# A state-space layer beside a gated feed-forward on one core: skip term from TensorE to VectorE, two chunks' layer norm from VectorE to ScalarE and GpSimd

## The chip, the core and the metric

The kernel runs on one core of a Trainium2 chip, in one launch. The metric is the device time of a run in microseconds (us). The engines are named as the profile names them: PE is TensorE (matmuls; PEld are its weight loads), DVE is VectorE, ACT is ScalarE, POOL is GpSimd, and SP is SyncE, which here only issues DMAs.

## The reference

The input `x` has 2048 rows (time steps) of 512 features. Each row is normalized to zero mean and unit variance, giving `xn`. Three things are added:

```
def _A_ref(x, ...):                       # called with xn
    Lam_bar = exp(dt * Lam)               # complex, one per state (512 states)
    Bu = einsum("bld,pd->blp", x, B_bar)
    for t in range(L): h = Lam_bar * h + Bu[:, t, :]
    y = 2.0 * einsum("blp,dp->bld", hseq, Cmat).real + x * Dskip
def _B_ref(x, w_gate, w_up, w_down):      # called with xn; F = 1376
    return (silu(x @ w_gate) * (x @ w_up)) @ w_down
return x + _A_ref(xn, ...) + _B_ref(xn, ...)
```

The part that the change is about is `x + xn * Dskip`, called the skip term here: per element one multiplication by a factor that depends on the feature alone, and one addition. Inputs, weights and the output are bf16.

## The kernel before

**Tiles and chunks.** A tile is 128 rows of `x`; there are 16 tiles (0 to 15) and four chunks of four tiles. `x_sb` holds all of `x` in SBUF for the whole run. `xn_sb` holds eight normalized tiles: tile a lies in slot a mod 8, so tiles 8 to 11 overwrite tiles 0 to 3. `xnT` holds the transposed normalized tiles of two chunks; chunk 2 overwrites chunk 0. PSUM has eight banks of 128x512 fp32, and `next_bank` hands out the one that has been idle longest. Every group of four 128x512 matmuls needs one bank, which comes free when ACT has copied the result to SBUF.

**Work of a chunk.** For a chunk c the functions do the following.

- `ln_chunk` normalizes its tiles. `ln_stats` lets DVE compute mean and variance (`bn_stats` L507, `bn_aggr` L509, plus eps L511) and POOL the power -0.5 (L513). In chunks 0 and 1 DVE then applies them (L518). In chunks 2 and 3 (`ln_norm_act`) DVE forms -mean*rstd (L522) and ACT applies both (L524, tasks xn8 to xn15).
- `xt_chunk_dma` transposes the chunk by one DMA on SP's queue (L407, tasks xTd1 to xTd3). Chunk 0 is transposed by PE. A DMA that transposes waits for all DMAs named before it in the code, and those named after it wait for it.
- `ssm_b_chunk` multiplies by B (L821); ACT copies the results to `u_sb` (L828, L830; tasks uev_re, uev_im).
- `ffn_gate` and `ffn_up` (L741) do 11 blocks of the hidden layer; ACT computes silu into `sg` (L754, six slots) and copies the other factor into `uf` (L805, three slots; tasks uev), and DVE multiplies them into `hT` (L807, tasks hmul).
- `ssm_elem_chunk` rotates, scans (L860) and rotates back on DVE, ending in `hss` (L875, tasks h).
- `wprep_C`, once, prepares the output matrix `W12` from C on ACT (L713, L715; tasks wev) and DVE (L717, L720).
- `dc_chunk` adds up the output of each tile in a PSUM bank: phase A is 11 matmuls of the down projection (L909, mm_dA), phase B eight matmuls of hss by W12 (L925, mm_dB). Then DVE adds what is left, into `osb` (L933 or L936, tasks oadd), and a DMA stores it.

**The skip term** is made in two ways. For tiles 0 to 7 (`rs_dve_from=8`) PE multiplies the transposed tile by a diagonal matrix of Dskip, four 128x128 matmuls more in phase A (L912); the diagonals `diagD` are built by DVE at the start from a row of Dskip that ACT's queue loads (L498). The last addition reads `x_sb` (L933). For tiles 8 to 15 `resid_tile` lets DVE compute `xn * dsk + x` in place in `xn_sb` (L596, L598; tasks rs1 and rs2) and the last addition reads `xn_sb` (L936). `dsk` is Dskip on all partitions, the last of the loads.

**The order on each engine.** The code names tasks with what they read and write. `_schedule` then lays them out before the launch: PE and SP keep the order of the code, while ACT, DVE and POOL get, again and again, the task that can start first; among those that can start within 200 ns of it the one with the longest path of costs to the end of the program. The costs are estimates in the code (`est=`); a DMA is reckoned with 2 us and its bytes at 330 per ns. The result is a fixed queue for each engine: an instruction whose data are late holds up all that stand behind it on that engine.

```
                ests = [(est_start(t, e), t) for t in cands]
                tmin = min(x[0] for x in ests)
                for (s_, t) in ests:
                    if s_ <= tmin + slack:
```

**The order of the code** around the change is: chunk 0's `ssm_elem_chunk`, `ln_chunk(2)`, `wprep_C`, all of chunk 1's matmuls, `ln_chunk(3)`, phase A of chunk 0, the transpose of chunk 2, phase B of chunk 0, then chunk 2's `ssm_b_chunk`, and so on with chunk 1's output and chunk 3. The transpose of chunk 2 stands behind phase A since the diagonal matmuls still read chunk 0 in `xnT`.

Of the kernel before, what the change touches and what calls it, by code (L numbers as in the profile page):

```python
# [24 lines left out]
    rs_dve_from=8,  # L25
# [226 lines left out]
def bass_parallel_sum__ssm_conv_s5__swiglu_ffn__prompt_kernel(  # L252
# [32 lines left out]
    with es:  # L285
        block = es.enter_context(nc.Block())

        def sb(name, shape, dt):
            return es.enter_context(nc.sbuf_tensor(name, shape, dt))
# [34 lines left out]
        wtmp = scrC[:, 0:2048].rearrange("p (k d) -> p k d", k=4)  # L324
        vq = sb("vq", [128, NU, 2, 2, CH], B16)
# [8 lines left out]
        praw = sb("praw", [128, 4, PT], B16)  # L334
        prow = sb("prow", [4, 4, 128], B16)
        ecst = sb("ecst", [128, PT], F32)
        diagD = sb("diagD", [128, KT, 128], B16)
# [85 lines left out]
        def pload(name, slot, src):  # L423
            dma(name, prow[:, slot, :], src.rearrange("(a p) -> a p", p=128), [("prow", slot)], 1024, eng="act")
# [3 lines left out]
        pload("ld_dskp", 3, A_Dskip)  # L428
# [57 lines left out]
        def params_t(ks):  # L486
            slot = next_tr()

            def tr(e, slot=slot):
                for k in ks:  # L490
                    inst = e.transpose(out=ptr[:, slot, 4 * k:4 * k + 4], in_=prow[0:4, k, :], identity=ident[0:4, 0:4])
                return inst
            g.add("pe", tr, reads=[("prow", k) for k in ks] + [("ident",)], writes=BK(slot), name="parT%d" % ks[0], est=30 * len(ks), ninst=len(ks))
            g.add("dve", lambda e, slot=slot: e.tensor_copy(out=praw[:, ks[0]:ks[-1] + 1].rearrange("p k a -> p (k a)"), in_=ptr[:, slot, 4 * ks[0]:4 * ks[-1] + 4]),
                  reads=BK(slot), writes=[("praw", k) for k in ks], name="parTev%d" % ks[0], est=80, prio=5000.0)
            if 3 in ks:
                for kt in range(KT):
                    g.add("dve", lambda e, kt=kt: e.tensor_scalar(out=diagD[:, kt, :], in0=ident[:], scalar1=praw[:, 3, kt:kt + 1], scalar2=None, op0=ALU.mult),  # L498
                          reads=[("praw", 3), ("ident",)], writes=[("diagD", kt)], name="diagD%d" % kt, est=90)
# [6 lines left out]
        def ln_stats(a, order=False):  # L506
            ln_bn[a] = g.add("dve", lambda e, a=a: e.bn_stats(out=st[:, a, :], in_=x_sb[:, a, :]),  # L507
                             reads=[("x", a)], writes=[("st", a)], name="bnst%d" % a, est=640)
            ln_ag[a] = g.add("dve", lambda e, a=a: e.bn_aggr(out=mv[:, a, :], in_=st[:, a, :]),  # L509
                             reads=[("st", a)], writes=[("mv", a)], name="bnag%d" % a, est=90)  # L510
            ln_ve[a] = g.add("dve", lambda e, a=a: e.tensor_scalar(out=ve[:, a:a + 1], in0=mv[:, a, 1:2], scalar1=EPS, scalar2=None, op0=ALU.add),  # L511
                             reads=[("mv", a)], writes=[("ve", a)], name="ve%d" % a, est=70)
            g.add("pool", lambda e, a=a: e.tensor_tensor(out=rstd[:, a:a + 1], in0=ve[:, a:a + 1], in1=mhalf[:, a:a + 1], op=ALU.pow),  # L513
                  reads=[("ve", a), ("mhalf",)], writes=[("rstd", a)], name="rstd%d" % a, est=600, prio=(3000.0 if a < 4 else 0.0))

        def ln_scale(a, norm_act):
            if not norm_act:
                ln_xn[a] = g.add("dve", lambda e, a=a: e.tensor_scalar(out=xn_sb[:, a % NXN, :], in0=x_sb[:, a, :], scalar1=mv[:, a, 0:1], scalar2=rstd[:, a:a + 1],  # L518
                                                                        op0=ALU.subtract, op1=ALU.mult),
                                  reads=[("x", a), ("mv", a), ("rstd", a)], writes=[("xn", a % NXN)], name="xn%d" % a, est=350)  # L520
            else:
                g.add("dve", lambda e, a=a: e.scalar_tensor_tensor(out=nmr[:, a:a + 1], in0=mv[:, a, 0:1], scalar=-1.0, in1=rstd[:, a:a + 1], op0=ALU.mult, op1=ALU.mult),  # L522
                      reads=[("mv", a), ("rstd", a)], writes=[("nmr", a)], name="nmr%d" % a, est=70)
                g.add("act", lambda e, a=a: e.activation(out=xn_sb[:, a % NXN, :], in_=x_sb[:, a, :], func=AF.Identity, scale=rstd[:, a:a + 1], bias=nmr[:, a:a + 1]),  # L524
                      reads=[("x", a), ("rstd", a), ("nmr", a)], writes=[("xn", a % NXN)], name="xn%d" % a, est=710)

        def ln_tile(a, norm_act):
            ln_stats(a)
            ln_scale(a, norm_act)

        def ln_head():
            for a in range(4):
                ln_stats(a)
            for a in range(4):
                ln_scale(a, False)
            seq = [ln_bn[0], ln_ag[0], ln_ve[0], ln_bn[1], ln_ag[1], ln_xn[0], ln_ve[1], ln_xn[1], ln_bn[2], ln_ag[2], ln_ve[2], ln_bn[3], ln_ag[3], ln_ve[3], ln_xn[2], ln_xn[3]]
            for p, q in zip(seq, seq[1:]):
                if p not in q.deps:
                    q.odeps.add(p)

# [6 lines left out]
        def ln_chunk(c):  # L547
            for a in range(4 * c, 4 * c + 4):
                ln_tile(a, _CFG["ln_norm_act"][c])
# [45 lines left out]
        def resid_tile(a):  # L595
            g.add("dve", lambda e, a=a: e.tensor_tensor(out=xn_sb[:, a % NXN, :], in0=xn_sb[:, a % NXN, :], in1=dsk[:], op=ALU.mult),  # L596
                  reads=[("xn", a % NXN), ("dsk",)], writes=[("xn", a % NXN)], name="rs1_%d" % a, est=340)
            g.add("dve", lambda e, a=a: e.tensor_tensor(out=xn_sb[:, a % NXN, :], in0=xn_sb[:, a % NXN, :], in1=x_sb[:, a, :], op=ALU.add),  # L598
                  reads=[("xn", a % NXN), ("x", a)], writes=[("xn", a % NXN)], name="rs2_%d" % a, est=340)
# [157 lines left out]
        def ffn_gate_quarters(c, tiles):  # L757
# [21 lines left out]
            params_t([0, 1, 2, 3])  # L779
# [111 lines left out]
        def dc_chunk(c, mid=None, split_last=False):  # L891
# [10 lines left out]
            for (lt, c0, nc_), bk in zip(items, banks):  # L902
                dg = (4 * c + lt < _CFG["rs_dve_from"])
                assert not (dg and nc_ != 512)

                def mmA(e, bk=bk, lt=lt, hb=hb, c=c, c0=c0, nc_=nc_, dg=dg):
                    for i in range(FT):
                        fs = fsz[i]
                        inst = e.matmul(pbank[:, bk, 0:nc_], lhsT=hT[0:fs, hb, i, lt * 128:(lt + 1) * 128], rhs=wd[0:fs, i, c0:c0 + nc_], start=(i == 0), stop=False)  # L909
                    if dg:  # L910
                        for kt in range(KT):
                            inst = e.matmul(pbank[:, bk, kt * 128:(kt + 1) * 128], lhsT=xnT[:, c % 2, lt, kt, :], rhs=diagD[:, kt, :], start=False, stop=False)  # L912
                    return inst
                g.add("pe", mmA, reads=[("hT", hb, i) for i in range(FT)] + [("wd", 0), ("wd", 1)] + (XN(c, lt) + [("diagD", kt) for kt in range(KT)] if dg else []),
                      writes=BK(bk), name="mm_dA%d_%d" % (4 * c + lt, c0), est=FT * (216 if nc_ == 512 else 110) + (KT * 60 if dg else 0), ninst=FT + (KT if dg else 0))
            if mid is not None:
                mid()
            for (lt, c0, nc_), bk in zip(items, banks):
# [13 lines left out]
                if a < _CFG["rs_dve_from"]:  # L932
                    g.add("dve", lambda e, bk=bk, a=a, os_=os_, c0=c0, nc_=nc_: e.tensor_tensor(out=osb[:, os_, 0:nc_], in0=pbank[:, bk, 0:nc_], in1=x_sb[:, a, c0:c0 + nc_], op=ALU.add),  # L933
                          reads=BK(bk) + [("x", a)], writes=[("osb", os_)], name="oadd%d_%d" % (a, c0), est=(660 if nc_ == 512 else 360))
                else:
                    g.add("dve", lambda e, bk=bk, a=a, os_=os_, c0=c0, nc_=nc_: e.tensor_tensor(out=osb[:, os_, 0:nc_], in0=pbank[:, bk, 0:nc_], in1=xn_sb[:, a % NXN, c0:c0 + nc_], op=ALU.add),  # L936
                          reads=BK(bk) + [("xn", a % NXN)], writes=[("osb", os_)], name="oadd%d_%d" % (a, c0), est=(660 if nc_ == 512 else 360))
# [20 lines left out]
        ssm_elem_chunk(0, u0)  # L958
        ln_chunk(2)
# [4 lines left out]
        for i in range(FT):  # L964
            ffn_gate(1, i)
            ffn_up(1, i)
        ln_chunk(3)
        dc_chunk(0, mid=lambda: xt_chunk_dma(2))
# [5 lines left out]
        dc_chunk(1, mid=lambda: xt_chunk_dma(3))  # L974
# [5 lines left out]
        for a in range(_CFG["rs_dve_from"], NT):  # L980
            resid_tile(a)
# [62 lines left out]
```

## Time and profile before

| | |
|---|---|
| time, median of 3 runs | 183.77 us (183.62 to 183.89) |
| the profiled execution's own time | 183.74 us |
| its span, first to last instruction | 182.0 us |
| granted clock of PE | 0.999 |
| busy: PE / DVE / ACT / POOL | 177.6 / 167.5 / 87.4 / 26.2 us |
| diagonal matmuls, L912 | 32, in eight sets of four |
| `bn_stats`, L507 | 16, 683 ns each |
| ACT applying the norm, L524 | 8, 803 ns each |
| DVE's skip term, L596 and L598 | 8 and 8, 418 and 419 ns each |

Times within the execution are counted from the first instruction. The mean duration of an instruction includes the part in which the next one on the same engine already runs, so the distance from one start to the next is shorter: eight results copied one after the other by ACT stand about 0.48 us apart, though each takes 0.6 us.

### The profile page before, as it was taken

What the parts mean: (1) busy time and instruction counts of PE and PEld (TensorE: products, weight loads), DVE (VectorE), ACT (ScalarE), POOL (GpSimd) and SP (SyncE); (2) the same over time, 40 slices, a digit from 0 to 9 for tenths busy, and PEclk for the clock granted to TensorE, in tenths of its full rate; (3) what the DMA queues carried; (4) which work ended last, traced back from release to release, by engine and by line L of the source; (5) the groups of instructions that cost most, each with busy time, mean ns of one, the idle gap of its engine ahead of it and who ended that gap; (6) DMA issues with size and microseconds to landing.
All of it is one profiled execution on the core that took longest, in us unless ns stands there. A gap on an engine that the chain in (4) does not pass through costs nothing.

```text
span 182.0 us, 2595 instructions
## 1 busy us (share of the span) xinstructions
PE 177.6 (98%) x943; PEld 87.0 (48%) x943; DVE 167.5 (92%) x359; ACT 87.4 (48%) x155; POOL 26.2 (14%) x37
## 2 busy tenths in 40 slices
PE   8899999999999999999999999999999999999994
PEld 3684444444444454444444455444444444444643
DVE  3799889999999998999999999999999999999933
ACT  3249987966798308057766480026667620000000
POOL 3597775000000004000000130000000000000000
PEclk9999999999999999999999999999999999999999
DMA  5993665669400000630000000620000000010202
GB/s 123 318 382 88 117 135 78 120 157 359 131 0 4 0 0 0 122 114 0 0 0 0 0 4 0 115 101 15 0 4 2 0 2 0 0 32 0 86 29 86
DMA packets 23404, 12.39 MB, mean 68 GB/s; under 512 B 15104, under 2 KB 23392, under 8 KB 23392
## 3 DMA queue, kind: packets, MB, share of 16 engines
q1 hardware_dynamic: 23360, 12.23, 25.3%
q8 instruction: 7, 0.11, 0.3%
q14 instruction: 5, 0.04, 0.1%
q10 hardware_dynamic: 32, 0.00, 0.0%
HBM read 6.46 MB, written 2.10 MB: 47 GB/s over the span
## 4 chain that ended last, share of the span: by engine, by line
PE 93%; DVE 3%; DMA 1%; POOL 1%; issue 0%; DVEq 0%
PE pb L741 39%; PE pb L909 21%; PE pb L925 15%; PE pb L821 15%; PE pb L768 1%; DMA x_sb<-in_A_x_dram 1%; DVE st L507 1%; PE pb L912 1%; DVE xn_sb L518 1%; POOL rstd L513 1%; POOL sm L643 1%; DVE mv L509 0%; DVE diagD L498 0%; DVE osb L936 0%; PE pb L580 0%
## 5 line engine op out<-in xcount | busy, mean ns | idle before, releaser
L741 PE MATMUL pb<-xnT,wu 128*128 128x512 bf16 (+1 forms) x176 | 43.7, 379 | 0.0
L909 PE MATMUL pb<-wd,hT 128*128 128x512 bf16 (+3 forms) x187 | 39.7, 367 | 0.0
L860 DVE TENSOR_TENSOR_SCAN vq<-sm,car,vq 128x512 bf16<-128x512 f32 x32 | 39.5, 1269 | 0.1
L741 PE MATMUL pb<-xnT,wg 128*128 128x512 bf16 (+1 forms) x152 | 38.4, 379 | 0.0
L805 ACT ACTIVATE uf<-pb 128x512 bf16<-128x512 f32 (+1 forms) x44 | 26.0, 605 | 16.1 <-DVE hT L807 9.3
L925 PE MATMUL pb<-W,hss 128*128 128x512 bf16 (+1 forms) x136 | 28.3, 366 | 0.0
L821 PE MATMUL pb<-xnT,BT 128*128 128x512 bf16 x128 | 28.1, 379 | 0.0
L741 PEld LDWEIGHTS pb<-xnT,wu 128*128 128x128 bf16 (+1 forms) x176 | 17.6, 100 | 20.1
L909 PEld LDWEIGHTS pb<-wd,hT 128*128 128x128 bf16 (+1 forms) x187 | 18.0, 98 | 18.5
L754 ACT ACTIVATE sg<-pb 128x512 bf16<-128x512 f32 (+1 forms) x38 | 22.6, 606 | 7.1 <-PE pb L741 6.9
L741 PEld LDWEIGHTS pb<-xnT,wg 128*128 128x128 bf16 (+1 forms) x152 | 15.3, 101 | 17.6
L513 POOL TENSOR_TENSOR rstd<-ve,mhalf 128x1 f32<-128x1 f32 x16 | 9.6, 616 | 76.1 <-DVE ve L511 76.1
L925 PEld LDWEIGHTS pb<-W,hss 128*128 128x128 bf16 x136 | 13.2, 98 | 13.9
L821 PEld LDWEIGHTS pb<-xnT,BT 128*128 128x128 bf16 x128 | 12.5, 98 | 15.1
L807 DVE TENSOR_TENSOR hT<-sg,uf 128x512 bf16<-128x512 bf16 (+1 forms) x44 | 18.4, 424 | 1.3 <-ACT uf L805 0.8
L828 ACT ACTIVATE u_sb<-pb 128x512 bf16<-128x512 f32 x16 | 9.5, 596 | 17.2 <-PE pb L821 17.2
L507 DVE BATCH_NORM_STATS2 st<-x_sb 128x6 f32<-128x512 bf16 x16 | 10.2, 683 | 3.0 <-DMA x_sb<-in_A_x_dram 3.0
L830 ACT ACTIVATE u_sb<-pb 128x512 bf16<-128x512 f32 x16 | 9.6, 598 | 3.2 <-PE pb L821 3.2
L866 DVE TENSOR_TENSOR scrA<-vq,cosT 128x1024 bf16<-128x1024 bf16 x16 | 10.9, 684 | 0.0
L870 DVE TENSOR_TENSOR scrA<-vq,sin 128x1024 bf16<-128x1024 bf16 x16 | 10.9, 684 | 0.0
L854 DVE TENSOR_TENSOR scrA<-u_sb,sin 128x1024 bf16<-128x1024 bf16 x16 | 10.9, 682 | 0.0
L851 DVE TENSOR_TENSOR scrA<-u_sb,cosT 128x1024 bf16<-128x1024 bf16 x16 | 10.9, 680 | 0.0
(74 smaller groups left out, 143.2 us busy)
## 6 DMA issues: line engine op xcount, KB each, us to landing
out_dram<-osb SPq DMA_DIRECT2D x15, 128.0 KB, 1.7
x_sb<-in_A_x_dram SPq DMA_DIRECT2D x3, 512.0 KB, 7.5
wd<-in_B_w_down_dram SPq DMA_DIRECT2D x1, 1280.0 KB, 7.1
wg<-in_B_w_gate_dram SPq DMA_DIRECT2D x2, 384.0 KB, 4.6
wu<-in_B_w_up_dram SPq DMA_DIRECT2D x1, 768.0 KB, 6.9
wg<-in_B_w_gate_dram SPq DMA_DIRECT2D x1, 608.0 KB, 7.9
wu<-in_B_w_up_dram SPq DMA_DIRECT2D x1, 608.0 KB, 9.0
x_sb<-in_A_x_dram SPq DMA_DIRECT2D x4, 128.0 KB, 3.0
```

Of the source, the lines that this page charges most:

```text
L507: ln_bn[a] = g.add("dve", lambda e, a=a: e.bn_stats(out=st[:, a, :], in_=x_sb[:, a, :]), reads=[("x", a)], writes=[("st", a)], name="bnst% ...
L513: g.add("pool", lambda e, a=a: e.tensor_tensor(out=rstd[:, a:a + 1], in0=ve[:, a:a + 1], in1=mhalf[:, a:a + 1], op=ALU.pow), reads=[("ve", ...
L741: inst = e.matmul(pbank[0:fs, bk, :].rearrange("p (j t) -> p j t", j=4), lhsT=w[:, kt, i * 128:i * 128 + fs], rhs=xnT[:, c % 2, :, kt, :], ...
L754: g.add("act", lambda e, sl=sl, bk=bk, fs=fs: e.activation(out=sg[0:fs, sl, :], in_=pbank[0:fs, bk, :], func=AF.Silu), reads=BK(bk), write ...
L805: g.add("act", lambda e, ul=ul, bk=bk, fs=fs: e.activation(out=uf[0:fs, ul, :], in_=pbank[0:fs, bk, :], func=AF.Identity), reads=BK(bk), w ...
L807: g.add("dve", lambda e, sl=sl, ul=ul, fs=fs, i=i, hb=hb: e.tensor_tensor(out=hT[0:fs, hb, i, :], in0=sg[0:fs, sl, :], in1=uf[0:fs, ul, :] ...
L821: inst = e.matmul(pbank[:, bk, :].rearrange("p (j t) -> p j t", j=4), lhsT=BT[:, ri, kt, pt * 128:(pt + 1) * 128], rhs=xnT[:, c % 2, :, kt ...
L851: g.add("dve", lambda e, sl=sl, U=U, Cb=Cb: e.tensor_tensor(out=pr2[:, sl, 0], in0=U, in1=Cb, op=ALU.mult), reads=ru + rdt, writes=[("pr", ...
L854: g.add("dve", lambda e, sl=sl, Usw=Usw, S2=S2: e.tensor_tensor(out=pr2[:, sl, 1], in0=Usw, in1=S2, op=ALU.mult), reads=ru + rdt, writes=[ ...
L860: g.add("dve", lambda e, sl=sl, ri=ri, pt=pt, rr=rr, c=c: e.tensor_tensor_scan(out=vq[:, sl, 1, ri, :], data0=rr[:, pt:pt + 1].to_broadcas ...
L909: inst = e.matmul(pbank[:, bk, 0:nc_], lhsT=hT[0:fs, hb, i, lt * 128:(lt + 1) * 128], rhs=wd[0:fs, i, c0:c0 + nc_], start=(i == 0), stop=F ...
L925: inst = e.matmul(pbank[:, bk, 0:nc_], lhsT=hss[:, hb, pt, ri, lt * 128:(lt + 1) * 128], rhs=W12[:, ri, pt, c0:c0 + nc_], start=False, sto ...
```

## The change

The diagonal matrices go, with their load, their building and the 32 matmuls. `resid_chunk` does the skip term of all 16 tiles on DVE, now with its sum written into `x_sb`, so all last additions read `x_sb`. Since chunk 2's tiles overwrite chunk 0's in `xn_sb`, chunk 0's skip term is named ahead of `ln_chunk(2)`, and chunk 1's ahead of `ln_chunk(3)`. In chunks 2 and 3 the sums come from ACT: one pass that adds up the tile, one that squares and adds up, both with a sum per row (`accum_out`) and a written tile `junk` that nobody reads; POOL does the small steps between, and ACT applies the norm as before. The transposes of chunks 2 and 3 are named ahead of `dc_chunk` and no longer in its middle.

```diff
-    rs_dve_from=8,
+        junk = sb("junk", [128, 512], B16)
-        diagD = sb("diagD", [128, KT, 128], B16)
-        pload("ld_dskp", 3, A_Dskip)
-            if 3 in ks:
-                for kt in range(KT):
-                    g.add("dve", ... diagD[:, kt, :] = ident * praw[:, 3, kt] ...)
...
+        def ln_tile_act(a):
+            jk = junk[:]
+            g.add("act", lambda e, a=a: e.activation(out=jk, in_=x_sb[:, a, :], func=AF.Identity, accum_out=mv[:, a, 0:1]),
+                  reads=[("x", a)], writes=[("mv", a), ("junk",)], name="lsum%d" % a, est=750)
+            g.add("pool", ... nmr = mv * (-1.0 / D) ...,           name="nmean%d" % a, est=150)
+            g.add("act", lambda e, a=a: e.activation(out=jk, in_=x_sb[:, a, :], func=AF.Square, bias=nmr[:, a:a + 1], accum_out=mv[:, a, 1:2]),
+                  reads=[("x", a), ("nmean", a)], writes=[("ss", a), ("junk",)], name="lsq%d" % a, est=750)
+            g.add("pool", ... ve = mv * (1.0 / D) + EPS ...,       name="ve%d" % a, est=150)
+            g.add("pool", ... rstd = ve ** mhalf ...,              name="rstd%d" % a, est=600)
+            g.add("pool", ... ve = nmr * rstd ...,                 name="nmr%d" % a, est=150)
+            g.add("act", ... xn_sb = rstd * x_sb + ve ...,         name="xn%d" % a, est=750)
...
-        def resid_tile(a):
+        def resid_chunk(c):
+            for a in range(4 * c, 4 * c + 4):
+                g.add("dve", ... xn_sb[:, a % NXN] = xn_sb[:, a % NXN] * dsk ..., name="rs1_%d" % a, est=340)
+                g.add("dve", ... x_sb[:, a] = x_sb[:, a] + xn_sb[:, a % NXN] ..., name="rs2_%d" % a, est=340)
...
-                    if dg:
-                        for kt in range(KT):
-                            inst = e.matmul(pbank[:, bk, kt * 128:(kt + 1) * 128], lhsT=xnT[:, c % 2, lt, kt, :], rhs=diagD[:, kt, :], start=False, stop=False)
...
         ssm_elem_chunk(0, u0)
+        resid_chunk(0)
         ln_chunk(2)
...
+        resid_chunk(1)
         ln_chunk(3)
-        dc_chunk(0, mid=lambda: xt_chunk_dma(2))
+        xt_chunk_dma(2)
+        dc_chunk(0)
...
-        dc_chunk(1, mid=lambda: xt_chunk_dma(3))
+        xt_chunk_dma(3)
+        dc_chunk(1)
...
-        for a in range(_CFG["rs_dve_from"], NT):
-            resid_tile(a)
+        resid_chunk(2)
+        resid_chunk(3)
         dc_chunk(2)
```

## The prediction

> **What bounds the kernel now.** I read the busy shares first, then the chain that ended last, then the queues of ACT, DVE and SP around chunk 2's norm and transpose.
>
> ```profile
> PE 177.6 (98%) x943; PEld 87.0 (48%) x943; DVE 167.5 (92%) x359; ACT 87.4 (48%) x155; POOL 26.2 (14%) x37
> PE 93%; DVE 3%; DMA 1%; POOL 1%; issue 0%; DVEq 0%
> ```
>
> PE is the bound: 93% of the chain is PE, and from 10.44 to 179.47 us it never stops. DVE is nearly as full, so it decides whether PE can stay so. ACT is half idle. In order of time the chain shows what the change removes, and when PE wants chunk 2's transposed tiles:
>
> ```profile
> 67.94 2.38 PE pb L909 x11
> 70.32 0.23 PE pb L912 x4
> 70.54 6.91 PE pb L925 x32
> 77.45 6.91 PE pb L821 x32
> ```
>
> Each set of four diagonal matmuls (L912) stands openly on the chain. L821 at 77.45 is the first reader of chunk 2 in `xnT`. SP's timeline shows how near that is to a wait:
>
> ```profile
> 38.41 0.37 SPq L412 DMA_DIRECT2D x_sb<-in_A_x_dram  x1
> ...
> 72.10 1.74 SPq L407 DMA_TRANSPOSE xnT<-xn_sb  x1
> 76.36 3.85 SPq L412 DMA_DIRECT2D out_dram<-osb  x4
> ```
>
> The transpose starts at 72.10, lands 4.2 us later, and the stores behind it go at 76.36: PE has 1.1 us to spare. ACT's and DVE's timelines show what the transpose waits for, and where this region begins:
>
> ```profile
> 37.72 0.60 ACT L830 ACTIVATE u_sb<-pb 128x512 bf16<-128x512 f32 x1 [0.27 <-PE pb L821]
> 38.59 0.60 ACT L828 ACTIVATE u_sb<-pb 128x512 bf16<-128x512 f32 x1 [0.27 <-PE pb L821]
> ...
> 58.31 0.72 ACT L713 ACTIVATE scrC<-hss,sm 128x512 f32<-128x512 bf16 x1
> 58.92 0.72 ACT L715 ACTIVATE scrC<-hss,sm 128x512 f32<-128x512 bf16 x1
> ...
> 68.98 2.93 ACT L524 ACTIVATE xn_sb<-x_sb,nmr,rstd 128x512 bf16<-128x512 bf16 x4
> ```
>
> ```profile
> 45.34 0.42 DVE L807 TENSOR_TENSOR hT<-sg,uf 128x512 bf16<-128x512 bf16 x1
> ...
> 46.88 0.42 DVE L807 TENSOR_TENSOR hT<-sg,uf 128x512 bf16<-128x512 bf16 x1
> ...
> 63.76 1.29 DVE L875 TENSOR_TENSOR hss<-scrA 128x1024 bf16<-128x1024 bf16 x2
> 64.97 2.47 DVE L507 BATCH_NORM_STATS2 st<-x_sb 128x6 f32<-128x512 bf16 x4
> ```
>
> Tiles 8 to 11 are normalized from 68.98 on, the transpose follows the last of them (71.91) by 0.19 us, and the norm waits for DVE, which turns to chunk 2's statistics at 64.97 only, after chunk 0's hss. Before phase B of chunk 0 (70.54) hss, ready at 65.05, has 5.5 us to spare.
>
> **The change, part by part.** *Diagonal matmuls.* Eight sets on the chain, 0.23, 0.23, 0.22, 0.23, 0.23, 0.23, 0.22 and 0.23 us: -1.82. Four stand before L821 of chunk 2, so PE would be there at 77.45 - 0.91 = 76.5.
>
> *Diagonals.* Three of DVE's four L498 stand before tile 3's norm (9.19 to 9.68). But that norm also waits for POOL's rstd, 8.96 + 0.60 = 9.56. So I take -0.05, not the 0.49 of the three. The load of a row of Dskip on ACT's queue delays nobody; without it nothing moves.
>
> *Skip term of chunks 0 and 1.* 16 instructions of 0.42 us, start to start 0.33, 2.7 us a chunk. They take the place of four statistics (2.47), the small L509 and L511 (0.46 together in starts), four L522 and the waits for POOL. Over the run DVE loses 16 x 0.42 = 6.7 of work more and 8 x (0.68 + 0.16 + 0.14 + 0.16) + 1.0 = 10.1 less, so it is no nearer to being the bound. If dsk came late they would stall; its row lands 7.3 us after 40.7, at 48, long before.
>
> *Norm on ACT, its place in the queue.* The layout rule gives ACT the first task that can start. By its reckoning of the loads tiles 8 to 11 are there at 37.2 of its clock, which is 0.8 behind the trace at this point: 38.0. So lsum8 goes into ACT's first gap after that, between the two evacuations shown at 37.72 and 38.59. From this reckoning I take the order only. In the trace the load starts at 38.41:
>
> ```profile
> x_sb<-in_A_x_dram SPq DMA_DIRECT2D x1, 512.0 KB, 3.6
> ```
>
> It lands 3.6 us later, at 42.0. ACT, which never waited here, will stand still from 38.3 to 42.0, and behind lsum8 are queued u_sb's and the feed-forward's evacuations. PE survives that: a group takes 0.863 us, its bank is wanted again eight groups later, so the group evacuated at 38.59 (begun at 37.69) must be out by 44.6 and is out at about 43.3. Cover: 1.3 us; beyond it, PE pays one for one.
>
> *Its size.* No row shows a pass with a sum. Below: the distance of evacuations back to back, 0.48, for lsum, and 0.61 (58.31 to 58.92, one operand from SBUF) for lsq, mean 0.54. Above: their full 0.61 and 0.73 and a further small ACT instruction (L638, 0.30) for the sum, mean 0.96. I take the middle, L = 0.75. `junk` and the means chain the passes strictly: lsum8, lsq8, lsum9 and so on.
>
> *What that does to DVE.* Up to DVE's second hmul of chunk 1 stand, from 42.0, four passes and eight evacuations: 42.0 + 4L + 7 x 0.48 + 0.65 = 49.0. Before, it started at 46.88: DVE loses 2.1 (1.3 to 3.0 over the bounds), after which it is the slower of the two again. hss of chunk 0 is ready at 67.2; PE needs it at 69.6: covered. Then come four rs1 and the first rs2, 1.75 us, and tile 8 may be normalized at 65.05 + 2.1 + 1.75 = 68.9.
>
> *What ACT itself allows.* By the same rule 24 evacuations, eight L713/L715 and 12 passes (chunk 2's eight, and four of tiles 12 and 13 that fill the gap) stand before tile 8's norm, with 0.9 us for round trips to POOL and for `junk`: 42.0 + 24 x 0.48 + 8 x 0.61 + 0.9 + 12L = 59.3 + 12L = 68.3 (65.8 to 70.8). POOL's small steps have no row; the nearest are a 128x1 MEMSET of 0.10 and the power, 0.54 to 0.85. Two of them lie open, so the upper bound adds 1.0; I took 0.35 each with hops, near the MEMSET since nothing there is a power. [...] The row: of the four powers at 67.84, beside DVE's hmul, one took 0.85 and three 0.54. [...]
>
> *Transposes.* Named earlier, chunk 2's no longer waits for phase A, but phase A was done at 70.54 and never was the last wait; on SP's queue nothing lies between the old place and the new. From tile 8's start the trace needs 2.93 + 0.19 + 4.2 = 7.3 us. The later of 68.9 and 68.3 gives 76.2 to 76.3: as before, not sooner, against PE at 76.5. Nearly nothing is left, so I add 0.1 us of waiting. The stores of chunk 0 behind it on SP have time: a bank is wanted only four groups after L821 begins.
>
> *Chunk 3.* Its passes fill ACT's gaps from 65 us on, its skip term follows chunk 1's hss at about 101, the transpose lands near 110, PE wants it at 118.9: free. The end is unchanged: the same eight tiles' skip terms, and the addition from `x_sb` costs what L936 cost.
>
> **Sum,** against the profiled execution's 183.74 (0.03 under the median): 183.74 - 1.82 - 0.05 + 0.1 = 181.97, so 182.0.
>
> **The rivals.** *Transposes late, gain partly lost.* From L = 0.82 (ACT's sum reaching 69.2) tile 8 is late, and each 0.1 more costs 1.2 us. At L = 0.85 to 0.95 this gives 182.3 to 183.6. For it: the sum's read-out is unknown. Against: ACT is idle 7.7 us before 68.30 in the old trace, room that the queue may use better than I think.
>
> *Slower: ACT sets the start of chunk 2.* One mechanism: passes so long, or POOL's steps so late, that tile 8 starts after 71.0; from there the wait at 77.45 eats the whole 1.87. At both upper bounds, L = 0.96 and POOL's 1.0, tile 8 starts at 71.8, PE waits 2.6: 184.5. An extra table load for the square would be of this kind: the trace has a single one (L464, 1.28 us) for silu, sine and identity, and two for each of four squares put 10 us ahead of tile 8, 191; ACT's row speaks against it, three functions sharing one load. [...]
>
> *The diagonals do not carry their time.* If PE's freed 1.82 us reappear as a wait elsewhere, at hss or at a late bank, the time stays within 0.37 of 183.74. Against: hss keeps 2.4 us, banks 1.3.
>
> **How the numbers follow.** The forecast, a wait of at most 0.4, 181.8 to 182.3: 0.52. Late transposes, 182.3 to 183.6: 0.22, of which 0.06 lies within 0.2% (0.37 us, about what the measurement can tell). Slower, 184.1 to 191: 0.20. Gain lost elsewhere: 0.06, of which 0.03 within, 0.02 slower, 0.01 faster. So faster 0.52 + 0.16 + 0.01 = 0.69, same 0.09, slower 0.22. The range runs from 181.7 to 184.1, leaving out most of the slower case and little below.
>
> **What would show it.** L912 and L498 are gone; PE's first L821 of chunk 2 begins near 76.5; ACT has a new wait for `x_sb`'s load of about 3.7 us near 38; DVE's second hmul of chunk 1 near 49; the transpose at 72, no sooner. A PE wait at L821 longer than 0.5, passes over 0.85 apart, more table loads, or a PE wait before 60 would make the forecast wrong.

## The result and the profile after

| | before | after |
|---|---|---|
| time, median of the runs | 183.73 us (183.62 to 183.89) | 191.25 us (189.22 to 193.39) |
| ratio after to before | | 1.0328 (1.0275 to 1.0382) |
| the profiled execution's own time, span | 183.74, 182.0 us | 190.33, 188.6 us |
| granted clock of PE | 0.999 | 0.982 |

Here and below a ratio leaves out runs more than 1.5% above the fastest of their kernel, so the one above compares 189.22 and 190.33 us with before, without 192.18 and 193.39. The change made the kernel 3.3% slower; I had forecast 182.0 us. The page of the profile after (busy share of each engine; the chain that ended last, by engine; the granted clock of PE in 40 equal slices):

```profile
PE 178.9 (95%) x902; PEld 86.1 (46%) x910; DVE 165.3 (88%) x339; ACT 97.0 (51%) x187; POOL 42.5 (23%) x61
PE 79%; POOL 7%; ACT 6%; DMA 3%; DVE 3%; issue 1%; SPq 0%; ACTq 0%
PEclk9999999999999999956999999999999999999999
```

PE is only 79% of the chain, where it was 93%. POOL, whose part was 1%, now has 7%, and PE's clock falls in two slices in the middle. The chain of waits in order of time (start, duration, what) shows the place:

```profile
64.40 7.41 POOL nmr L533
...
71.83 0.82 ACT junk L535 x2
...
74.61 2.83 ACT xn_sb L543 x4
...
77.64 4.25 DMA xnT<-xn_sb
...
81.94 9.97 PE pb L830 x32
```

L533 is a step on 128x1 numbers, tile 12's -mean. ACT waits for it with tile 12's second pass (L535); behind that pass stand, in ACT's queue, tile 13's passes and the norm of tiles 8 to 11 (L543), which need nothing of tile 12. The transpose of chunk 2 goes at 77.64 (72.10 before), and PE, ready for chunk 2 at 76.38, waits 5.56 us until 81.94. The windows of the 32 matmuls of L830 and of L821 that they were, first after, then before (length, busy time and instructions of PE, PEld, DVE, ACT and POOL, granted clock, DMA share, GB/s), add one more loss:

```profile
81.94:91.90 9.96, 9.96 (x33) 3.95 (x34) 9.46 (x17) 5.04 (x11) 0.95 (x3) 0.70 0.16 55
```

```profile
77.45:84.36 6.91, 6.91 (x33) 3.14 (x32) 6.84 (x12) 4.18 (x7) 0.00 (x0) 1.00 0.21 70
```

At a granted clock of 0.70 the same work took 3.06 us longer. So the sum is: diagonals -1.82, chunk 0 earlier by 0.18 (0.12 of it because the first `bn_stats` could start at 2.90 and not at 3.02, the rest where the diagonals' building stood), wait +5.56, clock +3.06: +6.6, the difference of the spans, 188.6 - 182.0.

What went on beside the 128x1 step of 7.43 us is seen in the timeline of after around it (start, duration, engine, line, operation; in brackets the idle time before and its cause):

```profile
64.19 0.20 POOL L541 TENSOR_TENSOR ve<-nmr,rstd 128x1 f32<-128x1 f32 x1
64.27 0.74 DVE L729 SCALAR_TENSOR_TENSOR W<-hss,sm,scrC 128x512 bf16<-128x512 bf16 x1
64.36 7.43 POOL L533 TENSOR_SCALAR nmr<-mv 128x1 f32<-128x1 f32 x1
64.93 1.28 DVE L884 TENSOR_TENSOR hss<-scrA 128x1024 bf16<-128x1024 bf16 x2
66.14 1.42 DVE L605 TENSOR_TENSOR xn_sb<-xn_sb,dsk 128x512 bf16<-128x512 bf16 x4
67.48 1.42 DVE L607 TENSOR_TENSOR x_sb<-x_sb,xn_sb 128x512 bf16<-128x512 bf16 x4
68.82 1.09 DVE L816 TENSOR_TENSOR hT<-sg,uf 128x512 bf16<-128x512 bf16 x3
...
71.03 0.68 DVE L860 TENSOR_TENSOR scrA<-u_sb,cosT 128x1024 bf16<-128x1024 bf16 x1
71.83 0.72 ACT L535 ACTIVATE junk<-x_sb,nmr 128x512 bf16<-128x512 bf16 x1 [8.01 <-POOL nmr L533]
```

POOL's step begins beside DVE's last `scalar_tensor_tensor` and ends 0.08 us after DVE has run out of data (71.71). In between DVE works without a pause through 16 instructions with two inputs from SBUF; the new skip term (L605, L607) is half of them. DVE ran dry because its next data (`uf`) stood in ACT's queue behind the waiting pass: its next product, at 77.94, had waited 6.23 us for ACT's `uf`. The two engines held each other up.

### The profile page after: what moved, and what is told of

Its sections match the earlier page's. It is cut to its first block, busy times and chain, and to the rows that moved or that the text cites. A ratio compares the mean times of both kernels' runs of the same rounds, so it can differ in the third digit from the quotient of the medians.

```text
span 188.6 us, 2556 instructions
## 1 busy us (share of the span) xinstructions
PE 178.9 (95%) x902; PEld 86.1 (46%) x910; DVE 165.3 (88%) x339; ACT 97.0 (51%) x187; POOL 42.5 (23%) x61
## 4 chain that ended last, share of the span: by engine, by line
PE 79%; POOL 7%; ACT 6%; DMA 3%; DVE 3%; issue 1%; SPq 0%; ACTq 0%
PE pb L750 35%; PE pb L830 16%; PE pb L915 15%; PE pb L926 11%; POOL nmr L533 4%; DMA xnT<-xn_sb 2%; ACT xn_sb L543 1%; PE pb L777 1%; ACT junk L535 1%; DMA x_sb<-in_A_x_dram 1%; DVE st L501 1%; ACT scrC L724 1%; POOL rstd L539 1%; ACT uf L814 1%; DVE xn_sb L511 1%
## 5 line engine op out<-in xcount | busy, mean ns | idle before, releaser
L915 PE MATMUL pb<-wd,hT 128*128 128x512 bf16 (+3 forms) x183 | 38.0, 366 | 0.2
L830 PE MATMUL pb<-xnT,BT 128*128 128x512 bf16 x128 | 31.0, 406 | 5.6 <-DMA xnT<-xn_sb 5.6
L830 PEld LDWEIGHTS pb<-xnT,BT 128*128 128x128 bf16 x128 | 13.2, 104 | 23.1 <-DMA xnT<-xn_sb 6.1
L933 DVE TENSOR_TENSOR osb<-pb,x_sb 128x512 bf16<-128x512 f32 (+1 forms) x17 | 11.1, 654 | 6.4 <-PE pb L926 5.9
L533 POOL TENSOR_SCALAR nmr<-mv 128x1 f32<-128x1 f32 x8 | 10.4, 1298 | 14.6 <-ACT junk L531 14.4
L535 ACT ACTIVATE junk<-x_sb,nmr 128x512 bf16<-128x512 bf16 x8 | 5.9, 743 | 9.8 <-POOL nmr L533 9.7
```

The lines of the kernel that those rows point to most:

```text
L533: g.add("pool", lambda e, a=a: e.tensor_scalar(out=nmr[:, a:a + 1], in0=mv[:, a, 0:1], scalar1=-1.0 / D, scalar2=None, op0=ALU.mult), read ...
L830: inst = e.matmul(pbank[:, bk, :].rearrange("p (j t) -> p j t", j=4), lhsT=BT[:, ri, kt, pt * 128:(pt + 1) * 128], rhs=xnT[:, c % 2, :, kt ...
```

## The experiments

The theories, as the expectations name them. **P**: POOL's step is shut out by DVE's run, and the order of ACT's queue carries the delay to chunk 2's norm. **A**: it is the load of ACT itself, 12 passes and 24 evacuations. **D**: it is the load of DVE. **T**: where the runs of a kernel scatter, it is the landing times of DMAs.

**1. Chunk 3's passes behind chunk 2's norm.** `act_xn` holds the norm's tasks.

```
 name="lsum%d" % a, est=750
+    , order=([act_xn[11]] if a == 12 else ())
```

> The changed kernel with one order more: ACT runs the passes of tiles 12 to 15 only after it has normalized tile 11. Theory P (port): POOL's 7.4 us step for tile 12 was shut out by DVE's run of instructions with two SBUF inputs, and it cost time only because ACT's queue had passes of tiles 12 and 13 ahead of chunk 2's norm. P expects tile 8's norm at 67.9 (DVE's first rs2 done), the transpose landing near 75.3, no wait of PE at chunk 2's first matmul (76.4), 181.7 us (181.5 to 182.2). Theory A (ACT load): the passes and the wait for x put ACT behind. A expects only the 2.7 us of four passes back and some of the slow clock, 186 to 187. Theory D (DVE load): the skip term in the middle of the run puts DVE behind. D expects 190, unchanged.

```profile
67.90 2.93 ACT L545 ACTIVATE xn_sb<-x_sb,ve,rstd 128x512 bf16<-128x512 bf16 x4 [4.74 <-DVE x_sb L609]
```

The profiled execution took 182.10 us: tile 8's norm at 67.90 waits for DVE's skip term (L609) and for nothing else, and PE has no wait for chunk 2. Of ten runs three took 182.0 to 182.3, near P's range, and seven 184.2 to 185.5, which no theory had; median of all ten 184.28, ratio 0.998 (0.994 to 1.002). The trace is of the first sort, so it does not show what the seven lose. POOL still has a long step, 6.33 us at 83.22, now of a later tile. So P's place is right, but the order alone does not bring the gain in each run.

**2. The mean without POOL.** The summing pass scales by -1/D and writes -mean itself; ACT's order is that of after.

```
-    activation(out=jk, in_=x_sb[:, a, :], func=AF.Identity, accum_out=mv[:, a, 0:1])
-    POOL: nmr = mv * (-1.0 / D)
+    activation(out=jk, in_=x_sb[:, a, :], func=AF.Identity, scale=-1.0 / D, accum_out=nmr[:, a:a + 1])
```

> The changed kernel with ACT's queue in the same order, but POOL's step between the two passes gone: the summing pass scales by -1/512 itself, so its sum is the negative mean. P expects no wait of ACT for POOL ahead of chunk 2's norm, though 12 passes still stand before it: tile 8's norm at 67.9, 181.7 us (181.5 to 182.3). A expects it unchanged, 189 to 191, since ACT has the same work. D expects it unchanged, 189 to 191.

Median 182.17 us (six of ten runs 181.9 to 182.2, four 183.5 to 183.9), ratio 0.995 (0.992 to 0.998). The timeline of this run:

```profile
64.44 8.30 POOL L535 TENSOR_SCALAR ve<-mv 128x1 f32<-128x1 f32 x1 [0.34 <-ACT junk L533]
...
67.68 2.93 ACT L541 ACTIVATE xn_sb<-x_sb,ve,rstd 128x512 bf16<-128x512 bf16 x4 [1.73 <-DVE x_sb L605]
```

POOL is shut out even longer, 8.30 us, now at the next step of tile 12 (`ve`), but no pass of ACT waits for that one before tile 8's norm, which starts at 67.68. The same passes, the same order, the same DVE: A and D fall. Nor did the four runs near 183.7, of which there is no trace, come near the 189 to 191 of A and D. The loss needs both the long step and a pass that waits for it.

**3 and 4. One half of the change each.** Skip term and transposes as changed, statistics by DVE as before; and the norm as changed, the rest as before.

```
 3:  ln_tile_act(a):  bn_stats, bn_aggr on DVE, power on POOL, nmr on DVE, norm on ACT   (as before)
 4:  before.py, with ln_tile_act in place of ln_tile for chunks 2 and 3
```

> Only the skip term and the transposes as changed, chunks 2 and 3 with DVE's statistics as before. P expects DVE's statistics (3.2 us) and skip term (2.7 us) one after the other before chunk 2's norm, and POOL's powers shut out beside the skip term: tile 11 done near 75, the transpose landing near 79.3, PE waiting about 3 us, 184.6 (183.5 to 186). A expects no loss without passes on ACT, 181.7. D expects more than the changed kernel, over 190, since DVE has more to do.

Median 185.24 us, ratio 1.008 (1.007 to 1.010), as P has it and neither A (181.7) nor D (over 190); the profiled execution, 188.06 us, met a lower clock besides (below). The skip term now stands ahead of chunk 2's statistics on DVE, as expected. The four powers of POOL, 2.40 us together in before (67.84 to 70.24), stretch to 4.75 beside it:

```profile
68.59 4.75 POOL L507 TENSOR_TENSOR rstd<-ve,mhalf 128x1 f32<-128x1 f32 x4 [37.02 <-DVE ve L505]
```

The first of the four alone takes 3.20 us, to 0.43 us after the skip term's end at 71.37; each of the others takes 0.55, with DVE waiting for it.

> Only the norm of chunks 2 and 3 as changed (passes on ACT, small steps on POOL), diagonal matmuls, skip term and transposes as before. The norm of chunk 2 then waits for no skip term and stands ahead of tile 12's passes on ACT. P expects it done by about 66, the transpose after phase A as before, 183.7 (183.4 to 184.3), and any long POOL step off the path. A expects ACT's load to show here as well, 186 or more. D expects 183.7.

Median 191.06 us, ratio 1.040 (1.037 to 1.043): a loss as large without the skip term of chunks 0 and 1. P had 183.7, since chunk 2's norm is early here (62.31); by the time alone A would be right (186 or more). The waits show P's mechanism in another place (timeline):

```profile
82.82 5.29 POOL L540 TENSOR_TENSOR ve<-nmr,rstd 128x1 f32<-128x1 f32 x1
...
88.15 0.81 ACT L542 ACTIVATE xn_sb<-x_sb,ve,rstd 128x512 bf16<-128x512 bf16 x1 [5.72 <-POOL ve L540]
...
89.50 1.89 PE L762 MATMUL pb<-xnT,wg 128*128 128x512 bf16 x4 [5.15 <-ACT u_sb L849]
```

A step of tile 15 is shut out by the rotation of chunk 2; ACT's norm of tile 15 waits, chunk 2's `u_sb` evacuations stand behind it, and PE waits 5.15 us for a bank. P holds in a place that I had not thought of.

**5. A gap in DVE's run.** After, with four 128x1 instructions between the products and the sums of chunk 0's skip term.

```
+    for i in range(4):  DVE: gapt[:, i:i + 1] = mhalf[:, 0:1] * 1.0     # after rs1_0..3, before rs2_0..3
```

> The changed kernel with four 128x1 instructions of DVE put between the first and the second half of chunk 0's skip term, 0.3 us of work more, ACT's queue as it was. P expects POOL's step for tile 12 to end at this break, near 67.7, so 3.2 us long and not 7.4; the step for tile 13 then starts at 69.3 and is shut out until DVE stops for want of data near 72. Tile 8's norm then starts near 73, the transpose lands near 80.2, PE waits 3.8 and not 5.6, and with some slow clock after it 187.5 us (186 to 188.7). A and D expect 190 or a little more, for DVE's added work.

```profile
64.18 3.27 POOL L534 TENSOR_SCALAR nmr<-mv 128x1 f32<-128x1 f32 x1
...
65.95 1.43 DVE L607 TENSOR_TENSOR xn_sb<-xn_sb,dsk 128x512 bf16<-128x512 bf16 x4
67.41 0.34 DVE L611 TENSOR_SCALAR gapt<-mhalf 128x1 f32<-128x1 f32 x4
...
67.78 1.43 DVE L614 TENSOR_TENSOR x_sb<-x_sb,xn_sb 128x512 bf16<-128x512 bf16 x4
...
69.28 0.34 POOL L534 TENSOR_SCALAR nmr<-mv 128x1 f32<-128x1 f32 x1
```

The step ends at the gap (67.45), after 3.27 us and not 7.43: what holds it is DVE's run. Median 183.4 us, ratio 0.999 (0.998 to 1.000), where I expected 187.5. Of ten runs seven took 183.3 to 183.8, the traced one among them, and three 186.9 to 187.5, as I had expected; of those there is no trace. In the traced one, behind the gap POOL's later steps, tile 13's at 69.28 among them (0.34), went through amid sums and products, the longest, a power, in 0.90 us; none was shut out a second time. That did not fit "two inputs from SBUF" as the reason. The gap holds two pauses as well: the four wait for the products (67.38 to 67.41) and the sums for the four (67.75 to 67.78). What a pause does is seen in run 11.

**6. Statistics first.** Run 2, with the passes of tiles 8 to 11 ahead of `wprep_C`'s on ACT where both can start.

```
+    prio=(1500.0 if a < 12 else 0.0)      # lsum and lsq
```

> The kernel without POOL's mean step (e2), and with the passes of tiles 8 to 11 ahead of W12's preparation in the layout's ranking, so that tile 11's last pass comes 2.8 us sooner. The runs of e2 fell into two groups, near 182.0 and near 183.8. P expects the second group to be runs in which tile 11's small steps on POOL miss their place before DVE's run of two-input instructions and are shut out; with tile 11 done by 60 all runs should lie near 181.8 (181.5 to 182.2). Rival T: the scatter comes from landing times of loads and transposes; T expects the same two groups, a median between 182.0 and 183.8.

Median 182.02 us (181.97 to 182.10), ratio 0.991 (0.9895 to 0.9925): the fastest kernel here, 1.7 us faster than before and at the forecast of the change. Tile 11's steps on POOL are done at 63.59 (64.09 in run 2's trace; I expected 60), ahead of DVE's long run, and none of the four runs lies near 183.8. Six of ten were near 182.0 in run 2 already, so four such runs come by chance about once in eight times, an estimate from that share; this speaks for P against T and does not decide it.

**7. The bare row.** A probe without the reference's work: rows of one DVE instruction, one POOL step in each.

> Only the disputed cost; the reference's work is left out and x is handed on as output. In each of eight stages DVE runs a row of equal instructions without a pause, and POOL, released by the second of them, runs one 128x1 multiplication from SBUF to SBUF. Stages: 16 additions of two 128x1024 bf16 tiles in SBUF; 16 products of two 128x512 bf16; 16 scalar_tensor_tensor with one bf16 and one fp32 input; 8 scans; 16 additions of a PSUM bank and a bf16 tile; 16 tensor_scalar; 16 bn_stats; and the first stage again with one 128x1 product as the eighth instruction. P expects POOL's step to last to the end of the row in stages 1 and 2 (near 8 us and 4.5 us), about one instruction in stages 3 and 4, under 0.5 us in 5 and 7, and to the small product, near 4 us, in 8; stage 6 is open. A and D expect about 0.2 to 0.9 us in every stage.

```profile
8.94 9.72 DVE L36 TENSOR_TENSOR o<-x_sb 128x1024 bf16<-128x1024 bf16 x16 [6.42 <-DMA x_sb<-in_A_x_dram]
...
10.41 0.50 POOL L78 TENSOR_SCALAR pq<-pv 128x1 f32<-128x1 f32 x1 [9.57 <-DVE o L36]
```

A miss for P: the step took 0.2 to 1.1 us in all eight rows, about what A and D had. Beside two-input instructions it got in where one of them ended (0.32 to 0.59), beside sums from PSUM and `bn_stats` sooner (0.21). P in its simple form is refuted: these rows of two-input instructions did not by themselves keep POOL out.

**8. What the bare row lacks.** Theories W, R, O and N are in the expectation.

> A probe of its own; the whole of the reference's work is left out. Nine rows of DVE instructions, all 128 partitions, bf16, two SBUF inputs each, and beside each a chain of five small POOL steps on 128x1. The rows: (0) 24 plain 128x512 products; (1) the same, each waiting for DVE's own instruction four back; (2) the same, each with a wait on ACT that was met long ago; (3) four products in place in xn, four sums in place in y that read them, three times; (4) and (5) 16 sums of 128x1024, each waiting for the instruction two back, and one back; (6) three 128x512 scalar_tensor_tensor, two sums of 128x1024, 16 products; (7) row 0, with POOL's steps released by ACT's summing passes; (8) the kernel's sequence around 64 us with its waits, POOL released by ACT. In the plain rows of the probe before, one POOL step took 0.2 to 1.1 us. Theory W (what shuts POOL out is that DVE's instructions have waits, or depend on each other): some of rows 1 to 5 hold a step for 4 us or more, row 0 and row 7 none. Theory R (it is how POOL's step is released: by ACT, in the middle of a DVE instruction): rows 7 and 8 hold steps for 4 us or more, rows 0 to 5 none. Theory O (the order of kinds of instruction: a step that begins beside a scalar_tensor_tensor and runs into plain two-input ones): rows 6 and 8 hold one. Theory N (something in the kernel that no row has): every step takes under 1.5 us, and what makes the run of two-input instructions close stays open.

```profile
11.34 0.24 POOL L105 TENSOR_SCALAR pv<-pv 128x1 f32<-128x1 f32 x1 [10.43 <-DVE o L42]
...
66.78 6.49 POOL L105 TENSOR_SCALAR pv<-pv 128x1 f32<-128x1 f32 x1 [8.08 <-DVE o L43]
```

Only row 6 (second line) holds a step, to 0.07 us after the row's end. Waits (rows 1 to 5: 0.23 to 0.66 us) and ACT as releaser (row 7: 0.23 to 0.51) did nothing: W and R fall; O is half right: what stands in front of the row matters, but row 8, the kernel's own sequence, held none: its first step got in just where the `scalar_tensor_tensor` ended, and those behind it took 0.2 to 0.5 us.

**9. The products as `scalar_tensor_tensor`.**

```
-    tensor_tensor(out=xn, in0=xn, in1=dsk, op=mult)
+    scalar_tensor_tensor(out=xn, in0=xn, scalar=1.0, in1=dsk, op0=mult, op1=mult)     # tiles 0 to 3
```

> After, with one edit: the four products of the skip term of chunk 0 are written as scalar_tensor_tensor with the scalar 1.0, still with two SBUF inputs and in place; every queue keeps its order. If any DVE instruction with two SBUF inputs keeps POOL out, POOL's step of tile 12 lasts as long as in after or longer, 7.4 to 8.8 us (the four products take some 0.66 us apart and not 0.33, 1.3 more in all), and the time is 191 to 193. If only tensor_tensor does (theory O's other half: the traces show small POOL steps of 0.9 to 1.0 us finishing beside scalar_tensor_tensor, at 63.16 in after), the step ends beside the first or second of the four, at 66.2 to 67.6, so it takes 1.9 to 3.2 us, as with the four small instructions of the run with the gap; the products cost DVE 1.3 us, tile 8's norm starts at 69.9 to 71.7, and the time is 183 to 185, or up to 187.5 where a later step of POOL falls into the sums behind.

```profile
64.54 8.50 POOL L533 TENSOR_SCALAR nmr<-mv 128x1 f32<-128x1 f32 x1
```

The step took 8.50 us (to 73.04) and the time is 191.91 us (189.78 to 194.35): these four opened nothing.

**10 and 11. The row taken apart.** Probes again, 21 and 17 rows.

> A probe of its own; all of the reference's work is left out. Row 6 of the probe before (three 128x512 scalar_tensor_tensor, two sums of 128x1024, 16 products of 128x512, no waits) held a 128x1 POOL step for 6.49 us, to its end; steps that came into rows of plain sums and products let in at the next boundary. Here 21 rows, two POOL steps each, the first released when a given number of the row's DVE instructions are done: rows 0 to 5 are that row again, released after 3, 2, 4, 5, 7 and 3; 6 and 7 have only sums, only products behind the three; 8 to 10 have no scalar_tensor_tensor; 11 has waits two back on the sums, 12 waits on ACT, long met, on all; 13, 18 and 19 have scans, tensor_scalar and sums from PSUM in front; 14 to 17 have one other instruction amid the products (scalar_tensor_tensor, tensor_scalar of 128x512 and of 128x1, a sum from PSUM); 20 is scalar_tensor_tensor alone. Theory K (the change of kind: a step that arrives by the first plain two-input instruction behind another kind stays out until another kind or a pause): rows 0, 5, 6, 7, 13, 19 hold it for 4 us or more, rows 2 to 4, 8 to 10 and 20 let it in within 1.1, rows 14 to 17 after 3 to 4. Theory H (phase: a step that misses one boundary by some tens of ns misses all): rows 0 and 5 differ, and long steps appear in rows of every sort. Theory Q (a wait opens the row): rows 11 and 12 let it in within 1.1 where rows 0 and 5 do not.

The timeline of POOL, six of the first steps: rows 0, 2, 4, 8, 14 and 19.

```profile
12.91 6.48 POOL L110 TENSOR_SCALAR pv<-pv 128x1 f32<-128x1 f32 x1 [12.01 <-DVE o L44]
...
31.27 5.89 POOL L110 TENSOR_SCALAR pv<-pv 128x1 f32<-128x1 f32 x1 [8.84 <-DVE o L42]
...
50.58 4.62 POOL L110 TENSOR_SCALAR pv<-pv 128x1 f32<-128x1 f32 x1 [4.13 <-DVE o L43]
...
82.31 0.52 POOL L110 TENSOR_SCALAR pv<-pv 128x1 f32<-128x1 f32 x1 [0.87 <-DVE o L42]
...
133.17 3.14 POOL L110 TENSOR_SCALAR pv<-pv 128x1 f32<-128x1 f32 x1 [2.25 <-DVE o L44]
...
174.94 0.52 POOL L110 TENSOR_SCALAR pv<-pv 128x1 f32<-128x1 f32 x1 [2.06 <-DVE o L48]
```

Behind `scalar_tensor_tensor`, scans or `tensor_scalar` (rows 0, 5 to 7, 13, 18) a step stayed out until the row ended, 5.9 to 6.5 us, and so did steps that came later into the row (rows 2 to 4: 5.89, 5.29, 4.62), which K had let in. Rows of sums and products alone (8 to 10) let it in at the next boundary (0.26 to 0.53), and so did sums from PSUM in front (19: 0.52), which K had closed. An instruction of another sort in the middle let one step in after 3.1 us (14 to 17), while the second stayed out to the row's end (2.64 to 3.25); only beside the sum from PSUM (17) the second went through too (0.19). Waits did not help (11, 12: 6.49), so Q falls; equal rows agree to 0.01 us, so H falls.

> A probe of its own; all of the reference's work is left out. 17 rows as in the probe before, whose rows behind scalar_tensor_tensor, scans and tensor_scalar kept POOL out to their end, let a step in at one such instruction in their middle, and never closed behind plain sums, from PSUM too. All those instructions read a factor per partition from SBUF; in the run with scalar_tensor_tensor in the skip term the factor was a constant, and they opened nothing. Rows: 0 the closed row again; 1 to 5 have in the middle scalar_tensor_tensor with a constant, tensor_scalar with constants (128x512, 128x1), a 128x4 product, a pause; 6 to 10 have in front scalar_tensor_tensor with a constant, tensor_scalar with constants (128x512, 128x1), 128x4 products, bn_stats; 11 a scan and one sum from PSUM; 12 a pause behind the three; 13 one scalar_tensor_tensor with a constant behind the three; 14 to 16 steps released beside the last of the three, of one, behind one. Theory V (the factor per partition opens and closes): rows 6 to 10 let the step in within 1.1 us, rows 1 to 4 hold it to their end, over 4. Theory K (any other kind does): rows 6 to 8 hold it, 1 to 4 let it in at the middle, near 3.1. Both: row 0 6.5, row 5 near 3.1, row 11 held, row 12 not.

The timeline of POOL: both steps of rows 3 and 5, the first of rows 6 and 13.

```profile
39.42 3.13 POOL L114 TENSOR_SCALAR pv<-pv 128x1 f32<-128x1 f32 x1 [2.26 <-DVE o L46]
42.63 2.64 POOL L115 TENSOR_SCALAR pv<-pv 128x1 f32<-128x1 f32 x1
...
55.70 3.14 POOL L114 TENSOR_SCALAR pv<-pv 128x1 f32<-128x1 f32 x1 [2.27 <-DVE o L46]
58.92 0.36 POOL L115 TENSOR_SCALAR pv<-pv 128x1 f32<-128x1 f32 x1
64.07 0.52 POOL L114 TENSOR_SCALAR pv<-pv 128x1 f32<-128x1 f32 x1 [4.79 <-DVE o L56]
...
120.80 6.49 POOL L114 TENSOR_SCALAR pv<-pv 128x1 f32<-128x1 f32 x1 [8.24 <-DVE o L56]
```

V is right in rows 1, 2 and 6 to 10: `scalar_tensor_tensor` and 128x512 `tensor_scalar` with constants neither opened a closed row (6.42, 6.02 us; row 13, one behind the three, 6.49) nor closed one (0.52 each), and 128x4 products and `bn_stats` in front closed none either (0.52, 0.51). V is wrong in rows 3 and 4: very short instructions in the middle, without such a factor, let one step in (3.13, 3.15), while the next stayed out again (2.64). A pause of DVE opened the row for good (row 5: 3.14, then 0.36; row 12: 0.65), which also fits the traced execution of run 5, where later steps went through. Row 11 was wrong by both theories (0.53), and rows 15 and 16 suggest why: a single instruction with a factor that began after a pause closed nothing (0.53). In row 14 a step released beside the last of the three got in where it ended (0.58), as in row 8 of run 8.

What these rows have in common: **where DVE had run several instructions with a factor per partition from SBUF and went on to two-input instructions without a pause, POOL's steps stayed out until DVE paused (4.62 to 6.49 us); another instruction with such a factor, or a very short one, let one step through (3.13 to 3.15), and a sum from PSUM let steps in beside it (3.14, then 0.19).** In the kernel the `scalar_tensor_tensor` of `wprep_C` (factor in `sm`) come directly ahead of the long run at 64.93; run 6's step at 59.79 ends, 2.47 us later, beside the next of them; run 9's products have a constant. Two things stay open. A step that began beside the last instruction with a factor got in behind it at 58.27 in after (0.56 us), and not at 64.36 (7.43). And why a step stayed out beyond the instruction that it began beside is not seen in a trace. A run with the products' factor in SBUF in the kernel's own skip term was planned and has no result, so no change to the kernel itself has tested the factor.

## Why the prediction was wrong

**The step that failed** is the bound on POOL's small steps. I took 0.35 us for each of two that lie open, at most 1.0 more for both, and one took 7.43 us. The nearest row, the four powers at 67.84 in before, was no test: there DVE had one product to do and then waited itself for POOL, so the longest run beside a power was a single instruction (timeline of before):

```profile
67.84 2.40 POOL L513 TENSOR_TENSOR rstd<-ve,mhalf 128x1 f32<-128x1 f32 x4 [37.22 <-DVE ve L511]
67.85 0.42 DVE L807 TENSOR_TENSOR hT<-sg,uf 128x512 bf16<-128x512 bf16 x1
...
68.73 0.16 DVE L522 SCALAR_TENSOR_TENSOR nmr<-mv,rstd 128x1 f32<-128x1 f32 x1 [0.46 <-POOL rstd L513]
```

The row showed POOL beside a DVE that pauses, and the change puts its steps beside one that does not. I bounded the size by the nearest duration without asking what DVE executes at that time, though the step on the skip term says it: hss and eight two-input instructions, one behind the other.

The plain rows of runs 7, 8, 10 and 11 show that a DVE without a pause is not enough: there a step took 0.2 to 0.7 us beside sums and products, up to the end of the instruction under way, and 0.21 in run 7 beside sums from PSUM. In the closed rows of runs 8, 10 and 11 it outlasted the instruction that it began beside; in run 8 it stayed out through all 18 sums and products (6.49 us). So no bound of one instruction's length for each step would have held either.

**The rival that came true** is "Slower: ACT sets the start of chunk 2", by its second half, POOL's steps so late that tile 8 starts after 71.0. Its chain (tile 8, transpose 3.1 us later, landing, PE) is the one in the profile; tile 8 started at 74.51 and not at 71.8. I gave it 0.20 and the range ended at 184.1.

**A term that the sum lacked** is PE's clock after a wait: 3.06 of the 8.6 us lost. Before had no wait of PE after 10.44 us, so no row of it could show this. In after the clock was 0.50 from 81.94 to 86.00 and 1.00 from 88.00 on. In run 4 a wait of 5.15 us was followed by a clock of 0.82 over 10.50 us; in run 3's profiled execution one of 2.69 us by 0.80 over 8.75 us (the three other runs of this kernel, without a trace, had mean clocks of 0.998 to 1.000); in run 5 one of 1.31 us was followed by no drop (7.07 us for 32 matmuls, as without a wait). For after, 0.70 over 9.96 us is what half speed for 6.0 us would give, an estimate from that row. Which waits are followed by a drop, and for how long, these few executions do not show.

**What held.** The diagonals carried their time (-1.82), PE was ready for chunk 2 at 76.38 (76.5), the order on ACT's queue was as worked out. ACT's wait for `x_sb` was 2.74 us (3.7), the passes with their read-out are 0.63 and 0.72 us apart from the next instruction, mean 0.67 (0.75), and the trace has a single table load of ACT (1.28 us, at 1.39), the square included:

```profile
40.88 0.63 ACT L531 ACTIVATE junk<-x_sb 128x512 bf16<-128x512 bf16 x1 [2.74 <-DMA x_sb<-in_A_x_dram]
41.42 0.19 ACT L531 ACTIVATION_READ_ACCUMULATOR junk<-x_sb 128x1 f32 x1
```

DVE's second hmul of chunk 1 came at 48.03 (49.0), hss of chunk 0 at 66.21 (67.2), and tile 8 could have started at 67.9, as run 1 did (68.9). With POOL's step off ACT's path (runs 2 and 6) the forecast is met: medians of 182.17 and 182.02 us against 182.0, though four of run 2's ten runs took 183.5 to 183.9. So apart from POOL's step, and the clock that followed the wait, the working stood; the sizes listed here were a little pessimistic.

## What to carry to other kernels

When a change puts small steps on an engine beside a busier one, look up what the busier one executes at that time, without a pause and behind what, and not only how long such a step takes elsewhere: the mean of a tile took POOL 0.22 to 7.43 us in after. In a fixed in-order queue, ask of each instruction that waits for another engine which urgent work stands behind it: here the mean of tile 12, which is transposed at 112.01 only, held up tiles 8 to 11, and to let ACT write the mean itself and to place the urgent statistics first turned a 3% loss into a 0.9% gain. PE's wait of 5.56 us was followed by 3.06 us more at a lower clock.

## What the runs showed of the hardware

- A 128x1 instruction of POOL (a power aside) took 0.19 us while DVE was idle, 0.2 to 0.7 beside plain two-input sums and products, and 2.6 to 8.5 us where it was held to the end of a row of them behind several DVE instructions with a factor per partition; it ended 0.05 to 0.08 us after DVE's last instruction.
- A pass of ACT with a sum per row is two instructions: 0.63 us (0.72 for the square with a bias) and a read-out of 0.19 us, of which 0.09 is open to the next instruction.
- After PE's wait of 5.56 us the 32 matmuls behind it ran at a granted clock of 0.70, 0.50 at first: 9.97 us for 6.91.
